# Attention scores of two head pairs in a row, and one pool of four accumulator banks, in a talking-heads attention, MoE and MLP kernel

## The chip, the cores and the metric

One core of a Trainium2 chip runs the whole kernel. The metric is device time in microseconds (us) of one execution; lower is better. Every instruction of an engine runs in the order in which the program holds it, so an engine that has to wait for one instruction also holds up all those behind it. TensorE (PE in the profile) multiplies into eight accumulator banks (PSUM); VectorE (DVE) and ScalarE (ACT) read the banks; SyncE's queue (SP) issues most DMAs.

## The reference

Three stages, one after the other. The change lies in the first.

```python
def _attn_ref(q, k, v, w_pre, w_post):            # B, H, S, D = 4, 12, 448, 64
    scores = np.matmul(q, k.transpose(0, 1, 3, 2)) / np.sqrt(64)
    scores = np.einsum('bhij,hg->bgij', scores, w_pre)      # heads mixed before
    attn = softmax(scores)                                   # max, exp, sum, divide
    attn = np.einsum('bhij,hg->bgij', attn, w_post)          # heads mixed after
    return np.matmul(attn, v)
# x = rows of all heads, (1792, 768); then
# moe:  expert = argmax(x @ w_gate) of 8; y = gate * relu(x @ w1[e]) @ w2[e]
# mlp:  h = y @ w_in; out = (h * cos(h)) @ w_out
```

## The kernel before

The attention works on 16 chunks `X` of queries: each of the four batches has three chunks of 120 rows and one of 88 (`CH`, L23). For a chunk, `qk(X, j)` makes the scores of the head pair `j` (heads 2j and 2j+1). Q and K are held transposed, one head of the pair on partitions 0 to 63 and the other on 64 to 127, each split into a high and a low part, so a pair takes six matmuls of 448 columns: three products (`KH,QH`, `KL,QH`, `KH,QL`), each for the two halves of the partitions, into two banks of the pool `pq`. Two copies (`brought`, L501) bring them to `SB[X]` in SBUF. A chunk has six such pairs.

When all twelve heads of a chunk lie there, blocks of ten rows (nine at the end) are taken with a DMA (`relay`, L258) that puts 10 rows x 12 heads on 120 partitions. A block is then mixed (`m`, L460, two matmul instructions since fp32 takes two), reduced (`nm`, L463), exponentiated (`E`, L467), scaled through the second mixing matrix (`kr`, L470 to L475), and mixed again and turned at once (`pa`, L481, eight instructions); a copy (L484) collects it in `AT`. There are 180 blocks. After a chunk's last block come its products with V (`px`, L304, two halves of 48 instructions), their transposes to rows (`pt`, L363), and for groups of chunks the gate logits (`pl`, L333) and the counting for the routing (`pq`, `plead`, L137). At the end of each batch the next batch's K and Q are turned (`heads`: `tp`, L183, then casts L515 and L517). Background pieces (`f`, `sq`, L1519 to L1535) narrow the MLP's weights beside it all.

The order of the attention's work on PE, DVE, ACT and SP is written out by a planner, `Plan`, when the kernel is built. Tasks are generators whose steps say which engine they run on and for how long, which slots they take and give (`q`, `m`, `o`, `v` are accumulator banks, two of each; `x` and `E` are SBUF buffers, five and three) and which events they need. `Plan.run` always takes the step that can start first, and among those that can start within 0.02 us on that engine the one of lowest rank. A step's instructions are put out in that order and stay in it. Scores take two `q` slots at once (`score`), and each copy gives one back; V products, transposes, logits and counting take `v`; a head's transposes take `q`. Tasks of scores have a rank some four to ten blocks ahead of the chunk that needs them.

Before the plan starts, a written-out prologue turns the first batch's K and Q (`turned`, with banks of three pools in turn) and makes the scores of chunk 0. After it, `between` runs the last chunk's products beside the first expert's.

Of the kernel before, what the change touches and what calls it, by code (L numbers as in the profile page):

```python
# [47 lines left out]
class Plan:  # L48
# [10 lines left out]
    def __init__(self, slots):  # L59
        self.free = {t: [0.0] * n for t, n in slots.items()}  # L60
        self.at, self.engine, self.pending = {}, {}, []
        self.now = self.reached = 0.0

    def add(self, rank, task, bg=False):
# [23 lines left out]
    def run(self):  # L88
        while self.pending:
            options = []  # L90
            for i, (order, rank, task, bg, t, step) in enumerate(self.pending):
                r = self.ready(t, step)
                if r is None:
                    continue
                for e, (hold, lat) in step["run"].items():
                    options.append((max(r, self.engine.get(e, 0.0)), order, hold, i, e, r, bg and rank > self.reached))
            assert options, [p[5] for p in self.pending]
            pick = None
            for o in sorted(options):
                start, order, hold, i, e, r, bg = o  # L100
                if bg and any(p[4] == e and not p[6] and p[5] < start + 0.7 * hold for p in options):
                    continue
                pick = o
                break
            pick = pick or min(options)

            start, e = pick[0], pick[4]
            same = [o for o in options if o[4] == e and o[0] <= start + 0.02 and (not o[6] or pick[6])]
            start, order, hold, i, e, r, bg = min(same, key=lambda o: (o[1], o[0]))
            order, rank, task, bg, t, step = self.pending.pop(i)  # L110
            hold, lat = step["run"][e]
            for tag in step.get("take", ()):
                self.free[tag].pop(0)
            self.now = start
            self.engine[e] = start + hold
            end = start + lat
            for tag in step.get("give", ()):
                self.free[tag] = sorted(self.free[tag] + [end])
            self.reached = max(self.reached, step.get("reached", 0.0))
            for ev in step.get("ends", ()):  # L120
                self.at[ev] = end
            self.go(rank, task, bg, end + self.HOP, e)

# [18 lines left out]
def attention(ctx, qctx, tc, q, k, v, w_pre, w_post, wg, xs, lg, ident, nb=4, side=None, route=None):  # L142
# [10 lines left out]
    sm = ctx.enter_context(tc.tile_pool(name="a_sm", bufs=4))  # L153
    pq = ctx.enter_context(tc.tile_pool(name="p_q", bufs=2, space=PS))
    pm = ctx.enter_context(tc.tile_pool(name="p_m", bufs=2, space=PS))
    po = ctx.enter_context(tc.tile_pool(name="p_o", bufs=2, space=PS))
    pv = ctx.enter_context(tc.tile_pool(name="p_v", bufs=2, space=PS))
    bal = Balance(nc)
# [18 lines left out]
    def turned(b, j, s, cs=slice(0, 4)):  # L177

        src = (KN, QN)[s][b, j]
        pool, tag = ((pm, "m"), (po, "o"), (pv, "v"))[(2 * j + s if cs.start == 0 else j) % 3] if b == 0 else (pq, "q")  # L180
        ps = pool.tile([128, 512], F32, tag=tag, name=f"tp{b}_{j}_{s}_{cs.start}")
        for c in range(4)[cs]:
            nc.tensor.transpose(ps[:, c * 112 : c * 112 + 112], src[:, c].rearrange("p a d -> p (a d)"), ident[:112, :112])  # L183
        return ps
# [70 lines left out]
    def relay(n):  # L255
        X, be, rs, m, M = geom(n)
        XR[n] = sk.tile([120, S], F32, tag="x", name=f"x{n}", bufs=5)
        nc.sync.dma_start(out=XR[n][:M], in_=SB[X][rs])  # L258

    def premix(n):  # L260
# [4 lines left out]
        nc.vector.reduce_max(nm[:M], ps[:M, :S], axis=AX.X, negate=True)  # L265
        e = wk.tile([120, S], F32, tag="E", name=f"E{n}", bufs=3)
        sg = sm.tile([120, 1], F32, tag="sg", name=f"sg{n}")
# [27 lines left out]
    def av_mm(X, half):  # L295
        b, c = chunks[X]
        n = CH[c][1]
        px = pv.tile([128, 3, 128], F32, tag="v", name=f"px{X}_{half}")
        for pr in range(3):
            for cc in range(4):  # L300

                for e in range(2):
                    g = 2 * (3 * half + pr) + e
                    nc.tensor.matmul(px[64 * e : 64 * e + 64, pr, :n], VN[b, g // 3][:, g % 3, cc], AT[X][:, cc, g, :n], start=(cc == 0), stop=(cc == 3))  # L304
        return px
# [21 lines left out]
    def logits_mm(Xs):  # L327

        pl = pv.tile([128, 512], F32, tag="v", name=f"pl{Xs[0]}")
        for cc in range(6):  # L330
# [12 lines left out]
    def logit_tiles(X):  # L343

        b, c = chunks[X]
        new = []
# [3 lines left out]
        if new:  # L350
            pt = pv.tile([128, 512], F32, tag="v", name=f"plt{X}")
            for i, t in enumerate(new):
                nc.tensor.transpose(pt[:, 8 * i : 8 * i + 8], LT[:, t * 128 % (2 * S) :][:, :128], ident[:8, :8])
            nc.vector.tensor_copy(lg[:, new[0] : new[-1] + 1].rearrange("p t e -> p (t e)"), pt[:, : 8 * len(new)])
            if route is not None:
                for t in new:
                    route.ready(t, pv, "v")

    def rows_mm(X, half):
        n = CH[chunks[X][1]][1]  # L360
        pt = pv.tile([128, 3, 128], F32, tag="v", name=f"pt{X}_{half}")
        for cc in range(3):
# [28 lines left out]
    def repeat():  # L391

        wps = pv.tile([128, 512], F32, tag="v", name="wps")
        nc.tensor.matmul(wps[:120, :24], rep.rearrange("p i h -> p (i h)"), wpp.rearrange("p j g -> p (j g)"), start=True, stop=True)
# [55 lines left out]

    plan = Plan({"q": 2, "m": 2, "o": 2, "v": 2, "x": 5, "E": 3, "kr": 4, "Sb": 1, "AT": 1, "W": 2, "sq": 2, "f": 2, "kn": 2, "qn": 2, "xr": 1, "xc": 4, "vn": 0})

    def block(n):
# [10 lines left out]
        yield dict(run={"ACT": (0.63, 0.76)}, later=-4, take=["E"], give=["m"])  # L464
        e = wk.tile([120, S], F32, tag="E", name=f"E{n}", bufs=3)
        sg = sm.tile([120, 1], F32, tag="sg", name=f"sg{n}")
# [21 lines left out]
    def score(X, j):  # L488
        b, c = chunks[X]
        on = [("K", b, j), ("Q", b, j)]  # L490
        if X >= 2:
            on += [("x", k) for k in range(first_of[X - 2], end_of[X - 2] + 1)]
        if j:
            on.append(("s", X, j - 1))
        yield dict(run=pe(0.7), take=["q", "q"], on=on, ends=[("s", X, j)])
        SC[X, j] = qk(X, j)

# [5 lines left out]
    def heads(b, j, s_):  # L503

        tag, src, t = (("kn", k, KN), ("qn", q, QN))[s_]
        yield dict(run=dma(4.0), take=[tag])
        load_pair(b, j, sk.tile([112, 4, 2, D], F32, tag=tag, name=f"{tag}{b}_{j}"), src, t)
        yield dict(run=pe(0.38), take=["q"], on=[("s", 4 * b - 1, j)])
# [15 lines left out]
    def products(X):  # L524
# [3 lines left out]
        for half in range(2):  # L528
            yield dict(run=pe(0.02 * n + 0.21), on=ats + [("V", b)], take=["v"] + (["xc"] if half == 0 else []), give=["AT"] if half else [], ends=[("av", X, half)])
            px = av_mm(X, half)  # L530
            eng = yield dict(run=copying(3 * n), give=["v"], ends=[("xc", X)] if half else [])
            av_out(X, half, px, by[eng])
        for half in range(2):
            yield dict(run=pe(0.33), take=["v"] + (["xr"] if half == 0 else []))
            pt = rows_mm(X, half)
            eng = yield dict(run=copying(384), give=["v"])
            rows_out(X, half, pt, by[eng])
# [3 lines left out]
    def gates(Xs):  # L541
        yield dict(run=pe(0.75), take=["v"], on=[("xc", X) for X in Xs])
        pl = logits_mm(Xs)
        for i, X in enumerate(Xs):
            b, c = chunks[X]
            i0, n, _ = CH[c]
            t0 = b % 2 * S + i0
            eng = yield dict(run=copying(n), give=["v"] if X == Xs[-1] else [])
            by[eng](LT[:, t0 : t0 + n], pl[32 * i : 32 * i + 8, :n])
# [3 lines left out]
        while state[0] is not None and (state[0] + 1) * 128 <= b * S + CH[c][0] + CH[c][1]:  # L553
            new.append(state[0])
            state[0] = next(tiles, None)
        yield dict(run=pe(0.1 * len(new)), take=["v"])
        pt = pv.tile([128, 512], F32, tag="v", name=f"plt{X}")
        for i, t in enumerate(new):
            nc.tensor.transpose(pt[:, 8 * i : 8 * i + 8], LT[:, t * 128 % (2 * S) :][:, :128], ident[:8, :8])
        yield dict(run=dve(0.2), give=["v"], ends=[("gates", X), ("xcs", X)])  # L560
        nc.vector.tensor_copy(lg[:, new[0] : new[-1] + 1].rearrange("p t e -> p (t e)"), pt[:, : 8 * len(new)])
        for t in new:
            if t >= NT - 1:
                continue
            kept, real = [], route.nc
            yield dict(run=dve(0.17), take=["v"])
            route.nc = Taken(real, kept)
            route.count(t, pv, "v")
            route.nc = real
            kept[0][1]()  # L570
            for i, (e, emit) in enumerate(kept[1:]):
                yield dict(run={"DVE": dve(0.2), "PE": pe(0.06)}[e][e] and ({"DVE": (0.12, 0.19)} if e == "DVE" else pe(0.06)), give=["v"] * (1 if t != TE - 1 else 2) if i == len(kept) - 2 else [])
                emit()
# [26 lines left out]
    for X in range(1, len(chunks)):  # L600
        n0, nb0 = first_of[X], CH[chunks[X - 1][1]][2]
        for j in range(H // 2):
            r = n0 - 4 - 8 * (X % 4 == 3) - (H - 2 - 2 * j) * (nb0 - 5) / H
            plan.add(r, score(X, j))
            for i in range(2):
# [1108 lines left out]
```

## Time and profile before

| | us |
|---|---|
| median of 3 runs | 1356.49 (1356.41 to 1357.92) |
| profiled execution, device time | 1357.03 |
| its span, first to last instruction | 1355.3 |
| attention's planned part, in the span | about 28 to 528 |
| PE busy in the span | 1323.2 (98%) |
| DVE busy | 1057.3 (78%) |
| ACT busy | 817.0 (60%) |

What lies around the span (1357.03 less 1355.3) is 1.7 us. PE's granted clock is at full speed from beginning to end (0.998 on average). A busy PE counts the modelled ends of matmuls that overlap, so the distances between starts say more than the busy time does.

### The profile page before, as it was taken

Reading aid. Unit: us, or ns where it says so; the run is one execution under the profiler, and the core shown is the slowest. Engines: PE = TensorE matmul, PEld = TensorE weight load, DVE = VectorE, ACT = ScalarE, POOL = GpSimd, SP = SyncE. Lnnn points to the kernel's source line nnn. Section 1 sums busy time; section 2 is a strip of 40 time slices with the busy share of each in tenths; the row PEclk is TensorE's granted clock in tenths of the full one; section 3 lists DMA queues with packets and bytes.
Section 4 is the critical chain, followed back from the end, with each engine's and each line's share of the span. In section 5 each row is a group of like instructions: output and inputs, shape, how many; then the busy total and the mean of one; then the engine's idle time right before and its main releaser. Section 6 shows DMA issues by size and latency. Waiting matters only on the chain.

```text
span 1355.3 us, 24788 instructions
## 1 busy us (share of the span) xinstructions
PE 1323.2 (98%) x8826; PEld 1079.0 (80%) x8826; DVE 1057.3 (78%) x2418; ACT 817.0 (60%) x1501; POOL 71.1 (5%) x67
## 2 busy tenths in 40 slices
PE   7999999999989999899999999999999999999997
PEld 4667676776767777799999999998888888888886
DVE  6877788788877887899999999897766666666663
ACT  5456565666656555788888889865444444444432
POOL 1000000000000000210000010011100020002001
PEclk9999999999999999999999999999999999999999
DMA  8558655865657557259465774365333343324201
GB/s 185 192 170 216 214 186 170 222 220 179 184 154 230 179 188 250 69 178 374 149 208 186 254 259 175 106 226 182 122 111 109 101 143 109 99 94 140 93 24 47
DMA packets 153280, 227.02 MB, mean 168 GB/s; under 512 B 55744, under 2 KB 115392, under 8 KB 153152
## 3 DMA queue, kind: packets, MB, share of 16 engines
q1 hardware_dynamic: 146816, 200.20, 46.0%
q0 software_dynamic: 3744, 18.09, 3.9%
q10 hardware_dynamic: 2592, 7.08, 1.3%
q8 instruction: 73, 1.20, 0.4%
q14 instruction: 55, 0.45, 0.1%
HBM read 217.87 MB, written 31.85 MB: 184 GB/s over the span
## 4 chain that ended last, share of the span: by engine, by line
PE 57%; DVE 0%; ACT 0%; issue 0%; POOLq 0%; POOL 0%; ACTq 0%
PE dh L1462 17%; PE op L1406 17%; PE yp L1221 10%; PE h L1187 10%; PE ph L1208 1%; PE px L1115 1%; PE dpt L1343 1%; ACT wh L1026 0%; DVE wl L1027 0%; POOLq L1709 0%; POOL out_dram L1415 0%; ACT dhs L1466 0%; ACT r L1429 0%; DVE xl L1125 0%; PE gspg L964 0%
## 5 line engine op out<-in xcount | busy, mean ns | idle before, releaser
L1027 DVE TENSOR_TENSOR wl<-r,wh 128x768 fp32r<-128x768 f32 (+1 forms) x246 | 249.1, 1060 | 13.3 <-ACT wh L1026 10.4
L1026 ACT CAST wh<-r 128x768 fp32r<-128x768 f32 (+1 forms) x246 | 224.0, 930 | 39.2 <-PE h L1187 30.3
L481 PEld LDWEIGHTS pa<-kr,E 120*112 120x112 f32 (+1 forms) x1440 | 164.6, 177 | 51.0 <-issue 36.5
L481 PE MATMUL pa<-kr,E 120*112 120x120 f32 (+1 forms) x1440 | 182.7, 270 | 3.3 <-DVE kr L475 2.6
L460 PE MATMUL m<-x,kpre 120*120 120x448 f32 x360 | 167.2, 557 | 1.0 <-ACT E L467 1.0
L1027 DVE TENSOR_TENSOR wil<-wi,wih 128x768 fp32r<-128x768 f32 x64 | 60.9, 952 | 134.1 <-ACT wih L1026 134.1
L1026 ACT CAST wih<-wi 128x768 fp32r<-128x768 f32 x64 | 53.7, 841 | 159.1 <-PE dh L1462 158.0
L463 DVE TENSOR_REDUCE nm<-m 120x1 f32<-120x448 f32 x180 | 111.6, 620 | 43.0 <-PE m L460 35.2
L467 ACT ACTIVATE E<-m,nm 120x448 f32<-120x448 f32 x180 | 114.5, 636 | 50.2 <-DVE nm L463 25.7
L1406 PE MATMUL op<-woh,gh 128*128 128x512 f32 x448 | 115.2, 338 | 0.0
L1406 PE MATMUL op<-woh,gl 128*128 128x512 f32 x448 | 114.6, 336 | 0.0
L1406 PE MATMUL op<-wol,gh 128*128 128x512 f32 x448 | 114.4, 336 | 0.0
L1462 PE MATMUL dh<-dxh,wih 128*128 128x512 f32 (+1 forms) x384 | 112.8, 369 | 0.0
L1462 PE MATMUL dh<-dxl,wih 128*128 128x512 f32 (+1 forms) x384 | 112.4, 367 | 0.0
L1462 PE MATMUL dh<-dxh,wil 128*128 128x512 f32 (+1 forms) x384 | 111.6, 367 | 0.0
L304 PEld LDWEIGHTS px<-AT,vn 112*64 112x64 f32 x1536 | 73.8, 137 | 14.9 <-issue 9.9
L1026 ACT CAST woh<-wo 128x768 fp32r<-128x768 f32 x64 | 53.3, 834 | 53.6 <-PE op L1406 51.4
L484 ACT COPY AT<-pa 112x480 f32<-112x480 f32 (+1 forms) x104 | 59.1, 569 | 39.4 <-PE pa L481 35.8
L1462 PEld LDWEIGHTS dh<-dxl,wih 128*128 128x128 f32 x384 | 70.2, 189 | 13.1
L304 PE MATMUL px<-AT,vn 112*64 112x120 f32 (+1 forms) x1536 | 80.4, 261 | 0.0
L1462 PEld LDWEIGHTS dh<-dxh,wil 128*128 128x128 f32 x384 | 69.8, 189 | 13.1
L501 ACT COPY S<-s 120x448 f32<-120x448 f32 (+1 forms) x104 | 54.3, 531 | 42.3 <-PE s L241 41.8
(276 smaller groups left out, 2575.0 us busy)
## 6 DMA issues: line engine op xcount, KB each, us to landing
r<-in_moe_w_dram SPq DMA_DIRECT2D x54, 1024.0 KB
r<-in_moe_w_dram SPq DMA_DIRECT2D x72, 768.0 KB
x<-S SPq DMA_DIRECT2D x172, 210.0 KB
wi<-wi SPq DMA_DIRECT2D x32, 768.0 KB
wo<-wo SPq DMA_DIRECT2D x32, 768.0 KB
W<-in_moe_w_in_dram SPq DMA_DIRECT2D x32, 384.0 KB
W<-in_moe_w_out_dram SPq DMA_DIRECT2D x32, 384.0 KB
ys<-y ACTq DMA_DIRECT2D x17, 384.0 KB
```

Source lines behind the costliest of these rows:

```text
L304: nc.tensor.matmul(px[64 * e : 64 * e + 64, pr, :n], VN[b, g // 3][:, g % 3, cc], AT[X][:, cc, g, :n], start=(cc == 0), stop=(cc == 3))
L460: nc.tensor.matmul(ps[:M, :S], kpre[:M, :M], x[:M], start=True, stop=True)
L463: nc.vector.reduce_max(nm[:M], ps[:M, :S], axis=AX.X, negate=True)
L467: last["act"] = nc.scalar.activation(e[:M], ps[:M, :S], AF.Exp, bias=nm[:M], scale=1.0, accum_out=sg[:M])
L481: nc.tensor.matmul(pa[:112, c, :120], e[:M, c * 112 : c * 112 + 112], kr[:M], start=True, stop=True)
L484: last["post"] = by[eng](AT[X][:, :, :, j0 : j0 + m], pa[:112, :, :120].rearrange("p c (g i) -> p c g i", i=10)[:, :, :, :m])
L1026: self.latest["A"] = nc.scalar.copy(hi, src).ins
L1027: self.latest["V"] = nc.vector.tensor_tensor(lo, src, hi.bitcast(F32), op=ALU.subtract).ins
L1187: self.nc.tensor.matmul(hp[n], a[:, k], w[:, n * 512 : n * 512 + 512], start=(k == 0 and i == 0), stop=(k == 5 and i == 2))
L1221: self.nc.tensor.matmul(yp[n][:, :384], a[:, k], w[:, n * 384 : n * 384 + 384], start=(k == 0 and i == 0), stop=(k == 7 and i == 2))
L1406: nc.tensor.matmul(bank[:, to], g[:, t * P : t * P + P], w[:, of], start=first, stop=(f == 15 and i == 2), skip_group_check=(n == 1))
L1462: nc.tensor.matmul(hp[:, :N], w[:, k], x[:, k, :N], start=(k == 0 and i == 0), stop=(k == 5 and i == 2))
```

## The change

Four things.

1. Scores are made by a task for two head pairs, `j` and `j + 1`, with two steps. The first step is planned as 0.9 us, the second as 0.6 us if it follows the first directly on PE (`then`). `Plan` remembers the task whose first step PE ran last (`self.row`) and gives that task's second step the lead among the PE steps that can start at once. Where its two banks aren't free at that moment, another PE step goes in between and the second pair runs alone, as before. The task now needs K and Q of both pairs.
2. The pool `pv` is gone; `pq` has four banks, for scores, turned heads, V products, transposes, logits and counting alike. `between` takes its banks there too.
3. The prologue's turned tiles use the pools `pm` and `po` in turn, four banks, and not the six of `pm`, `po` and `pv`.
4. The relayed blocks `x` have six buffers and not five, the exponentials `E` four and not three.

```diff
@@ Plan
+        self.row = None
...
-            start, order, hold, i, e, r, bg = min(same, key=lambda o: (o[1], o[0]))
+            start, order, hold, i, e, r, bg = min(same, key=lambda o: (e != "PE" or self.pending[o[3]][2] is not self.row, o[1], o[0]))
             order, rank, task, bg, t, step = self.pending.pop(i)
             hold, lat = step["run"][e]
+            if e == "PE":
+                if self.row is task:
+                    hold, lat = step["then"], step["then"] + lat - hold
+                self.row = task if "then" in step and self.row is not task else None
...
-            self.go(rank, task, bg, end + self.HOP, e)
+            self.go(rank, task, bg, start + hold if self.row is task else end + self.HOP, e)
@@ attention
-    pq = ctx.enter_context(tc.tile_pool(name="p_q", bufs=2, space=PS))
+    pq = ctx.enter_context(tc.tile_pool(name="p_q", bufs=4, space=PS))
...
-    pv = ctx.enter_context(tc.tile_pool(name="p_v", bufs=2, space=PS))
@@ turned
-        pool, tag = ((pm, "m"), (po, "o"), (pv, "v"))[(2 * j + s if cs.start == 0 else j) % 3] if b == 0 else (pq, "q")
+        pool, tag = ((pm, "m"), (po, "o"))[(s if cs.start == 0 else j) % 2] if b == 0 else (pq, "q")
@@ relay, block
-        XR[n] = sk.tile([120, S], F32, tag="x", name=f"x{n}", bufs=5)
+        XR[n] = sk.tile([120, S], F32, tag="x", name=f"x{n}", bufs=6)
-        e = wk.tile([120, S], F32, tag="E", name=f"E{n}", bufs=3)
+        e = wk.tile([120, S], F32, tag="E", name=f"E{n}", bufs=4)
@@ the planner's slots; every take and give of "v" becomes "q", every pv a pq
-    plan = Plan({"q": 2, "m": 2, "o": 2, "v": 2, "x": 5, "E": 3, ...})
+    plan = Plan({"q": 4, "m": 2, "o": 2, "x": 6, "E": 4, ...})
@@ score(X, j)
-        on = [("K", b, j), ("Q", b, j)]
+        on = [(t, b, i) for t in "KQ" for i in (j, j + 1)]
...
-        yield dict(run=pe(0.7), take=["q", "q"], on=on, ends=[("s", X, j)])
-        SC[X, j] = qk(X, j)
+        for i in (j, j + 1):
+            yield dict(run=pe(0.9), then=0.6, take=["q", "q"], on=on, ends=[("s", X, i)])
+            SC[X, i] = qk(X, i)
@@ the tasks of scores
-            plan.add(r, score(X, j))
+            if j % 2 == 0:
+                plan.add(r, score(X, j))
```

## Rows read from the trace of the kernel before

**Rows 1.** The page, part 1: span, and each engine's busy us, share and instructions

```profile
span 1355.3 us, 24788 instructions
...
PE 1323.2 (98%) x8826; PEld 1079.0 (80%) x8826; DVE 1057.3 (78%) x2418; ACT 817.0 (60%) x1501; POOL 71.1 (5%) x67
```

**Rows 2.** Stages of the planned attention: window, us, busy us (x) of PE, PEld, DVE, ACT, POOL

```profile
28.00:528.00 500.00, 489.06 (x4242) 351.55 (x4243) 399.67 (x1316) 293.97 (x723) 1.21 (x2) 1.00 0.63 194
28.00:148.00 120.00, 115.51 (x929) 81.70 (x928) 96.94 (x282) 69.66 (x171) 0.00 (x0) 1.00 0.63 191
```

**Rows 3.** Waits of PE from 28 to 528 us, longest first: us, times, longest

```profile
PE tp L183 <- DMA qn<-in_q_dram: 2.7, 2, 2.4
PE pa L481 <- DVE kr L475: 2.6, 3, 1.6
```

**Rows 4.** Timeline of PE, 200 to 206 us: start, us, line, out<-in, xcount

```profile
200.62 1.76 PE L460 MATMUL m<-x,kpre 120*120 120x448 f32 x4
202.22 0.98 PE L481 MATMUL pa<-kr,E 120*112 120x120 f32 x8
203.13 0.47 PE L241 MATMUL s<-KH,QH 64*120 64x448 f32 x2
203.44 0.37 PE L241 MATMUL s<-KL,QH 64*120 64x448 f32 x2
203.64 0.37 PE L241 MATMUL s<-KH,QL 64*120 64x448 f32 x2
203.94 1.07 PE L481 MATMUL pa<-kr,E 120*112 120x120 f32 x8
204.85 0.92 PE L460 MATMUL m<-x,kpre 120*120 120x448 f32 x2
205.70 0.43 PE L241 MATMUL s<-KH,QH 64*88 64x448 f32 x2
```

**Rows 5.** Timeline of PE's weight loads at the same pair of heads

```profile
203.23 0.18 PEld L241 LDWEIGHTS s<-KL,QH 64*120 64x120 f32 x2
```

**Rows 6.** Groups by line, 28 to 528 us: the copies of scores; busy us, mean ns, idle before

```profile
L501 ACT COPY S<-s 120x448 f32<-120x448 f32 (+1 forms) x101 | 52.7, 531 | 39.5 <-PE s L241 39.0
L501 DVE COPY S<-s 120x448 f32<-120x448 f32 (+1 forms) x74 | 45.9, 621 | 12.6 <-PE s L241 9.1 <-DMA qn<-in_q_dram 1.0
```

**Rows 7.** Timeline of all engines at the plan's beginning, 21 to 28 us

```profile
21.39 1.37 PE L183 MATMUL tp<-ident,fq 112*128 112x112 f32 x12
...
22.21 1.88 DVE L202 TENSOR_TENSOR QL<-tp,QH 128x224 fp32r<-128x224 f32 x6
...
22.69 0.47 PE L241 MATMUL s<-KH,QH 64*120 64x448 f32 x2
...
24.18 0.46 PE L241 MATMUL s<-KH,QH 64*120 64x448 f32 x1 [0.62 <-ACT S L501]
...
26.26 0.75 PE L241 MATMUL s<-KH,QH 64*120 64x448 f32 x2 [0.42 <-ACT S L501]
...
27.35 1.76 PE L460 MATMUL m<-x,kpre 120*120 120x448 f32 x4
```

**Rows 8.** Timeline of all engines around one counting tile, 187 to 194 us

```profile
187.97 0.18 PE L137 MATMUL pq<-ohb,tri 128*128 128x8 bf16 x1
...
188.94 2.68 PE L304 MATMUL px<-AT,vn 112*64 112x120 f32 x48
...
193.28 0.49 PE L363 MATMUL pt<-ident,xc 128*120 128x128 f32 x3
...
193.48 0.29 DVE L137 TENSOR_TENSOR pa<-pq,pa 112x128 f16<-112x128 f32 x1 [0.18 <-PE pq L137]
```

**Rows 9.** Timeline of SP's queue at the end of the attention

```profile
516.65 0.33 SPq L1535 DMA_DIRECT2D wo<-f  x1
517.20 1.99 SPq L1091 DMA_DIRECT2D r<-in_moe_w_dram  x3
```

More of the change, by code (lines that the diff above doesn't have):

```diff
@@ L297, in av_mm @@
         n = CH[c][1]
-        px = pv.tile([128, 3, 128], F32, tag="v", name=f"px{X}_{half}")
+        px = pq.tile([128, 3, 128], F32, tag="q", name=f"px{X}_{half}")
         for pr in range(3):
@@ L327, in logits_mm @@
     def logits_mm(Xs):
-        pl = pv.tile([128, 512], F32, tag="v", name=f"pl{Xs[0]}")
+        pl = pq.tile([128, 512], F32, tag="q", name=f"pl{Xs[0]}")
         for cc in range(6):
@@ L350, in logit_tiles @@
         if new:
-            pt = pv.tile([128, 512], F32, tag="v", name=f"plt{X}")
+            pt = pq.tile([128, 512], F32, tag="q", name=f"plt{X}")
             for i, t in enumerate(new):
@@ L356, in logit_tiles @@
                 for t in new:
-                    route.ready(t, pv, "v")
+                    route.ready(t, pq, "q")
     def rows_mm(X, half):
         n = CH[chunks[X][1]][1]
-        pt = pv.tile([128, 3, 128], F32, tag="v", name=f"pt{X}_{half}")
+        pt = pq.tile([128, 3, 128], F32, tag="q", name=f"pt{X}_{half}")
         for cc in range(3):
@@ L391, in repeat @@
     def repeat():
-        wps = pv.tile([128, 512], F32, tag="v", name="wps")
+        wps = pq.tile([128, 512], F32, tag="q", name="wps")
         nc.tensor.matmul(wps[:120, :24], rep.rearrange("p i h -> p (i h)"), wpp.rearrange("p j g -> p (j g)"), start=True, stop=True)
@@ L449, in dma @@
         return {"SP": (0.8, d)}
-    plan = Plan({"q": 2, "m": 2, "o": 2, "v": 2, "x": 5, "E": 3, "kr": 4, "Sb": 1, "AT": 1, "W": 2, "sq": 2, "f": 2, "kn": 2, "qn": 2, "xr": 1, "xc": 4, "vn": 0})
+    plan = Plan({"q": 4, "m": 2, "o": 2, "x": 6, "E": 4, "kr": 4, "Sb": 1, "AT": 1, "W": 2, "sq": 2, "f": 2, "kn": 2, "qn": 2, "xr": 1, "xc": 4, "vn": 0})
     def block(n):
@@ L464, in block @@
         yield dict(run={"ACT": (0.63, 0.76)}, later=-4, take=["E"], give=["m"])
-        e = wk.tile([120, S], F32, tag="E", name=f"E{n}", bufs=3)
+        e = wk.tile([120, S], F32, tag="E", name=f"E{n}", bufs=4)
         sg = sm.tile([120, 1], F32, tag="sg", name=f"sg{n}")
@@ L506, in heads @@
         yield dict(run=dma(4.0), take=[tag])
-        load_pair(b, j, sk.tile([112, 4, 2, D], F32, tag=tag, name=f"{tag}{b}_{j}"), src, t)
+        load_pair(b, j, sk.tile([112, 4, 2, D], F32, tag=tag, name=f"{tag}{b}_{j}", bufs=2), src, t)
         yield dict(run=pe(0.38), take=["q"], on=[("s", 4 * b - 1, j)])
@@ L528, in products @@
         for half in range(2):
-            yield dict(run=pe(0.02 * n + 0.21), on=ats + [("V", b)], take=["v"] + (["xc"] if half == 0 else []), give=["AT"] if half else [], ends=[("av", X, half)])
+            yield dict(run=pe(0.02 * n + 0.21), on=ats + [("V", b)], take=["q"] + (["xc"] if half == 0 else []), give=["AT"] if half else [], ends=[("av", X, half)])
             px = av_mm(X, half)
-            eng = yield dict(run=copying(3 * n), give=["v"], ends=[("xc", X)] if half else [])
+            eng = yield dict(run=copying(3 * n), give=["q"], ends=[("xc", X)] if half else [])
             av_out(X, half, px, by[eng])
         for half in range(2):
-            yield dict(run=pe(0.33), take=["v"] + (["xr"] if half == 0 else []))
+            yield dict(run=pe(0.33), take=["q"] + (["xr"] if half == 0 else []))
             pt = rows_mm(X, half)
-            eng = yield dict(run=copying(384), give=["v"])
+            eng = yield dict(run=copying(384), give=["q"])
             rows_out(X, half, pt, by[eng])
@@ L541, in gates @@
     def gates(Xs):
-        yield dict(run=pe(0.75), take=["v"], on=[("xc", X) for X in Xs])
+        yield dict(run=pe(0.75), take=["q"], on=[("xc", X) for X in Xs])
         pl = logits_mm(Xs)
@@ L547, in gates @@
             t0 = b % 2 * S + i0
-            eng = yield dict(run=copying(n), give=["v"] if X == Xs[-1] else [])
+            eng = yield dict(run=copying(n), give=["q"] if X == Xs[-1] else [])
             by[eng](LT[:, t0 : t0 + n], pl[32 * i : 32 * i + 8, :n])
@@ L555, in gates @@
             state[0] = next(tiles, None)
-        yield dict(run=pe(0.1 * len(new)), take=["v"])
-        pt = pv.tile([128, 512], F32, tag="v", name=f"plt{X}")
+        yield dict(run=pe(0.1 * len(new)), take=["q"])
+        pt = pq.tile([128, 512], F32, tag="q", name=f"plt{X}")
         for i, t in enumerate(new):
             nc.tensor.transpose(pt[:, 8 * i : 8 * i + 8], LT[:, t * 128 % (2 * S) :][:, :128], ident[:8, :8])
-        yield dict(run=dve(0.2), give=["v"], ends=[("gates", X), ("xcs", X)])
+        yield dict(run=dve(0.2), give=["q"], ends=[("gates", X), ("xcs", X)])
         nc.vector.tensor_copy(lg[:, new[0] : new[-1] + 1].rearrange("p t e -> p (t e)"), pt[:, : 8 * len(new)])
@@ L565, in gates @@
             kept, real = [], route.nc
-            yield dict(run=dve(0.17), take=["v"])
+            yield dict(run=dve(0.17), take=["q"])
             route.nc = Taken(real, kept)
-            route.count(t, pv, "v")
+            route.count(t, pq, "q")
             route.nc = real
@@ L571, in gates @@
             for i, (e, emit) in enumerate(kept[1:]):
-                yield dict(run={"DVE": dve(0.2), "PE": pe(0.06)}[e][e] and ({"DVE": (0.12, 0.19)} if e == "DVE" else pe(0.06)), give=["v"] * (1 if t != TE - 1 else 2) if i == len(kept) - 2 else [])
+                yield dict(run={"DVE": dve(0.2), "PE": pe(0.06)}[e][e] and ({"DVE": (0.12, 0.19)} if e == "DVE" else pe(0.06)), give=["q"] * (1 if t != TE - 1 else 2) if i == len(kept) - 2 else [])
                 emit()
```

## The prediction

> **What bounds the kernel now.** I read the page's busy shares first: PE is busy for 98% of the span, DVE for 78% [rows 1]. Then the stages: from 28 to 528 us, the planned attention, PE is busy for 489.1 of 500 us, DVE for 399.7, ACT for 294.0 [rows 2]. With 180 blocks in it that is 2.78 us a block, of which PE fills 2.72, DVE 2.22 and ACT 1.63. PE would have to lose about a fifth of its work before DVE could set the pace. Next PE's waits in that stage: the longest sums are 2.7 us for DMAs of the next batch's Q and 2.6 us for `kr` [rows 3]; no long sum is a wait for an accumulator bank. So what PE loses there lies inside its own stream, and the view that shows it is the timeline of starts.
>
> There one pair of heads stands between a `pa` and a `pa` [rows 4]: its three products start at 203.13, 203.44 and 203.64, and the next work at 203.94. The middle product takes 0.20 us, the first 0.31, the last 0.30. So 0.81 us are spent on what would be 0.60 at the pace of the middle step. The entry costs a bit more: `m` before scores takes 0.85 (204.85 to 205.70), while two `m` before a `pa` take 1.60 together (200.62 to 202.22), 0.80 each; a `pa` before scores takes 0.91 (202.22 to 203.13), no more than the 0.91 before an `m` (203.94 to 204.85). The planner of before had two banks for scores, so a pair always stood alone: all 87 pairs from 28 us on pay this.
>
> **The change, part by part.**
>
> *Two pairs in a row.* If the second pair runs at the middle step's pace through its entry, and the first pair's exit too, the pair of pairs saves the excess of one first step (0.11), of one last step (0.10) and, where the second pair would have stood behind an `m`, that entry's 0.05, say half the time: 0.24 us. Nothing in the trace shows two pairs in a row, so bounds. From below: if the second pair's first loads can't run ahead, its first step stays at 0.31 and 0.13 is saved. From above 0.26, with the `m` entry every time. I take 0.24, since within a pair each product's loads already run while the product before streams: the loads for the second product start at 203.23, 0.10 us after the first matmul and 0.21 before their own [rows 4, 5].
>
> A rule that speaks against this: the Trainium skill, TensorE: Matmul & The Clock Gate, section "Part 3: Packing small matmuls — row/col tiling", says that a weight load overlaps a running matmul only when it goes to another group of rows. By that rule the second pair's first load would wait for the half it goes into, the price would be the lower bound, and the time that of the third rival below; the row at 203.23 speaks against it, as both halves are streaming then.
>
> *How many.* There are 15 planned chunks with three pairs of pairs each, 45; three of them are chunk 1's, counted with the beginning below, so 42. Each second pair needs two more free banks just when the first ends. What else holds banks: scores until their copies are done (0.53 us on ACT, 0.62 on DVE, two at once [rows 6]); a half of V's products for 2.6 us and its copy (188.94 to 191.55 by the distance to the next start; the row at 188.94 lasts 2.68); a counting tile from 187.97 to 193.77, 5.8 us [rows 8], of which there are 13. With one tile of another kind in use three banks are left, and the second pair must wait or go alone. Blocks leave about 5 us between two pairs of pairs, long enough for the four copies. I estimate 85% in a row, 36; bounds 50% and 100%. Sum: 36 x 0.24 = 8.6 us, all of it on PE, which is the path here.
>
> *Four banks at the beginning.* After the prologue PE makes chunk 1's scores and waits for copies: pairs start at 22.69, 24.18 and 26.26 us, and the first `m` at 27.35 [rows 7]. Three pairs at 0.81 fill 2.4 of 4.7 us. With four banks one to three more pairs fit into the 2.3 us of gaps, or the first `m` comes earlier, where its DMA allows. I take 1.5 us, bounds 0 and 2.5.
>
> *Fewer banks for the prologue.* The six late transposes (21.39 to 22.69) go into four banks, so the fifth waits for the first's reader on DVE, which starts at 22.21 and takes 0.31 each (1.88 for six) [rows 7]. PE would be held to about 22.9 with chunk 1's scores and the first `m` queued behind it. The 2.3 us of gaps hide that; without them it would cost 0.3 to 0.6 us. I take 0.
>
> *One pool for all.* Does a counting tile block the tiles behind it when banks are shared? It need not, as one stretch shows [rows 8]: with two banks in `pv`, both the half of V's products at 188.94 and the transposes at 193.28 run while the counting tile is still held (its last reader starts at 193.48). So a bank is taken as it comes free, not in turn. Cost 0; the other case is the slower rival.
>
> *More `x` and `E` buffers.* They can only take away waits, and PE is idle for 10.9 us in the stage [rows 2]. The named waits are for Q's DMA and `kr` [rows 3]; neither needs these buffers. I take 0, bounds 0 and 3 us of gain. SP's queue issues the same DMAs; relays may go out one earlier.
>
> *What comes after.* The first expert's weights are issued at 517.20, right after SP's last piece of the attention at 516.65 [rows 9]: they hang on the attention's order, not on a time of their own, and come forward with it. After that, PE is the chain that ends last, so the gain arrives in full.
>
> Sum: 8.6 + 1.5 = 10.1 us. The profiled execution's 1357.0 becomes 1346.9; it stands 0.5 above the median, so I forecast 1346.5. Ends: 21 x 0.13 = 3 us, and 42 x 0.26 + 2.5 + 3 = 16.4 us.
>
> **The rivals.**
>
> *Few in a row.* The change may not do what it says. If V's halves, turned heads and counting hold a bank whenever a pair of pairs comes up, a third of the 42 are in a row: 14 x 0.24 + 1.5 = 4.9 us, 1351.6. For it speaks that all four banks must be free or about to be; against it that scores are planned blocks ahead and can choose their moment.
>
> *The gain is given back.* The order of everything is planned anew, and PE keeps to it. Where PE waits for DMAs, as in the first 120 us of the stage with 4.5 us idle [rows 2], being earlier is worth nothing. If half the gain is lost there and the 10.9 us of idle time become 15, the gain is 1 us: about 1355.5.
>
> *No load ahead.* The lower price: 36 x 0.13 + 1.5 = 6.2 us, 1350.3.
>
> *Slower: PE stands for banks.* Some 110 tiles that had `pv` or `pq` with little company (30 halves, 30 transposes, 36 turned heads, 13 countings) now share with 45 pairs of pairs that take all four banks. PE's order is fixed by planned durations; where a copy comes later than planned, PE stands with `m` and `pa` of the next blocks behind it, and DVE and ACT then stand for those. Such a wait can be as long as one copy, 0.53 to 0.62 us [rows 6]. It decides from a mean of 0.12 us a tile (13 us, more than the gain and 2.7). At 0.15, 16.5 us go and the time is 1357 - 10 + 16.5 = 1363. Against it: at most 10.9 us were idle with two banks of each kind, and a shared pool of four gives each kind more than it had on average. The Trainium skill, TensorEngine Tiling, section "Gotcha 1: PSUM Pressure", warns of just this: row tiles raise the pressure on the banks.
>
> **How the numbers follow.** Forecast 0.55, at 1340.5 to 1350; no load ahead 0.10; few in a row 0.13; given back 0.11; slower 0.11. A measurement of this kernel can tell about 0.2%, 2.7 us, from no change. The first three are faster: 0.78. Given back is within: 0.11. Slower: 0.11. The range holds the first three and about half of the fourth: from 1340 (about the upper end of the gain, 16.4 us) to 1355.5.
>
> **What would show it.** In the timeline after: twelve score matmuls in a row with starts 0.20 us apart across the seam (right), or 0.31 again (no load ahead). The count of such rows: 36 or so of 45, or a third. PE's waits: no sum of more than 3 us with `S` copies or `xc` copies as the releaser; if those grow to over 10 us, the slower rival holds. At the beginning: no wait for `S` between 22 and 27 us. The distance from the first `m` to the first expert's first hidden matmul should shrink by 8 to 10 us, and all behind it stay as it is. The prediction is wrong if that distance doesn't shrink, or if it does and the end doesn't follow.

## The result, and the profile after

| | us |
|---|---|
| before, median of 4 | 1356.61 |
| after, median of 4 (1339.77 to 1346.05) | 1343.28 |
| ratio, 95% interval | 0.9893 (0.9878 to 0.9909) |
| profiled execution after, device time | 1346.05 |
| its span | 1343.3 |

The kernel is 13.3 us faster by the medians. The profiled execution of after is the longest of its four, 11.0 us under the profiled one of before; the readings below are from it. Its span is 12.0 us shorter; what lies around the span is 2.7 us here and was 1.7 in before. One execution of all, of the kernel before in another order, took 7434 us and is left out of the ratios.

Page of after, part 1, as [rows 1]:

```profile
span 1343.3 us, 24789 instructions
...
PE 1312.6 (98%) x8826; PEld 1084.1 (81%) x8826; DVE 1056.0 (79%) x2427; ACT 814.1 (61%) x1492; POOL 74.0 (6%) x67
```

PE's busy time has fallen by 10.6 us, DVE's by 1.3 and ACT's by 2.9. Timeline of PE in after around two tasks of scores (start, us, line, out<-in, xcount), as [rows 4]:

```profile
44.64 0.46 PE L245 MATMUL s<-KH,QH 64*120 64x448 f32 x2
44.94 0.37 PE L245 MATMUL s<-KL,QH 64*120 64x448 f32 x2
45.14 0.36 PE L245 MATMUL s<-KH,QL 64*120 64x448 f32 x2
45.35 0.36 PE L245 MATMUL s<-KH,QH 64*120 64x448 f32 x2
45.55 0.37 PE L245 MATMUL s<-KL,QH 64*120 64x448 f32 x2
45.75 0.36 PE L245 MATMUL s<-KH,QL 64*120 64x448 f32 x2
46.05 1.07 PE L485 MATMUL pa<-kr,E 120*112 120x120 f32 x8
46.96 0.92 PE L464 MATMUL m<-x,kpre 120*120 120x448 f32 x2
47.71 0.98 PE L485 MATMUL pa<-kr,E 120*112 120x120 f32 x8
48.53 0.92 PE L464 MATMUL m<-x,kpre 120*120 120x448 f32 x2
...
53.25 0.92 PE L464 MATMUL m<-x,kpre 120*120 120x448 f32 x2
54.10 0.47 PE L245 MATMUL s<-KH,QH 64*120 64x448 f32 x2
```

Two pairs take 1.41 us (44.64 to 46.05), where two single ones took 1.62. The seam, 45.14 to 45.35, runs at the middle step's pace: the loads for the matmuls at 45.35 start at 45.15, while both halves stream.

```profile
45.15 0.18 PEld L245 LDWEIGHTS s<-KH,QH 64*120 64x120 f32 x2
```

And there is more to read here than the prediction read. The `pa` right behind scores takes 0.91 (46.05 to 46.96), the `pa` between two `m` 0.82 (47.71 to 48.53). The `m` between two `pa` takes 0.75 (46.96 to 47.71), the `m` ahead of scores 0.85 (53.25 to 54.10). So each change between the half-height tiles of the scores (64 of the array's 128 rows, 64*120 in their rows) and full-size work costs 0.09 us in the neighbour too, on the way in and on the way out.

In the planned part of after, 30 of 42 tasks have their pairs in a row and 12 do not; chunk 1's three tasks all stand ahead of the first `m`. Timeline of PE at the beginning of after, as [rows 7]:

```profile
22.48 0.56 PE L245 MATMUL s<-KH,QH 64*120 64x448 f32 x2
...
24.16 0.46 PE L245 MATMUL s<-KH,QH 64*120 64x448 f32 x1 [0.43 <-DVE S L506]
...
24.67 0.56 PE L245 MATMUL s<-KH,QH 64*120 64x448 f32 x2
...
26.26 0.56 PE L245 MATMUL s<-KH,QH 64*120 64x448 f32 x2
...
27.16 1.01 PE L464 MATMUL m<-x,kpre 120*120 120x448 f32 x2
```

Six pairs are made by 27.16 us, where before made three by 27.35. PE still stands for a copy of scores once, 0.43 us at 24.16. PE's waits from 28 to 518 us in after (us in total, times, longest), as [rows 3]:

```profile
PE tp L187 <- DMA qn<-in_q_dram: 6.1, 4, 3.4
PE m L464 <- DMA x<-S: 1.5, 1, 1.5
...
PE s L245 <- DVE l L142: 0.7, 1, 0.7
...
PE s L245 <- ACT S L506: 0.4, 1, 0.4
```

The waits for banks are short. The long one is for the landing of Q of the last batch, 3.4 us in one piece, more than in before (2.4).

To set work against waits I summed distances between starts for the planned part, from the first `m` to the end of the last `pa` of a block. The work, called own work below, is counted at the undisturbed distances: 180 blocks at 0.754 + 0.820; a half of V's products 2.61 (1.97 in short chunks); turned heads 0.385, transposes 0.33, logits 1.34; a pair alone 0.80 (0.77 in short chunks), two in a row 1.41 (1.38 in short chunks); and 0.094 for each change between full-size work and scores, V's products or logits. V's products are half as wide (112*64 in their rows) and logits 8 columns wide (128*8); a `pa` ahead of logits takes 0.914 and an `m` ahead of V's products 0.845, as ahead of scores. The small matmuls of the counting, 2 to 3 us in all, are in it too. What is left of the stretch is put down as wait, slower work at a lower clock included.

| profiled execution of | pairs, and runs of two | changes | own work, us | waits, us | last `pa` ends at |
|---|---|---|---|---|---|
| before | 87, 0 | 218 | 480.6 | 18.8 | 526.8 |
| after | 84, 30 | 164 | 467.1 | 22.0 | 516.3 |

The own work falls by 13.5 us: the three pairs that the beginning has taken in (0.80 and two changes each, 3.0) and 30 pairs in a row (10.5, so 0.35 each). The waits grow by 3.2, most of it slower work at a lower clock (2.8 us, shown in the last section). From the first hidden matmul of the first expert to the MLP's first it is 328.3 us before and 326.8 after, a further 1.5 us gained.

### The profile page after: what moved, and what is told of

Its sections match the earlier page's. It is cut to its first block, busy times and chain, and to the rows that moved or that the text cites. A ratio compares the mean times of both kernels' runs of the same rounds, so it can differ in the third digit from the quotient of the medians.

```text
span 1343.3 us, 24789 instructions
## 1 busy us (share of the span) xinstructions
PE 1312.6 (98%) x8826; PEld 1084.1 (81%) x8826; DVE 1056.0 (79%) x2427; ACT 814.1 (61%) x1492; POOL 74.0 (6%) x67
## 4 chain that ended last, share of the span: by engine, by line
PE 58%; DVE 1%; issue 0%; ACT 0%; POOLq 0%; POOL 0%; ACTq 0%
PE dh L1468 17%; PE op L1412 17%; PE yp L1227 11%; PE h L1193 10%; PE ph L1214 1%; PE px L1121 1%; PE dpt L1349 1%; DVE wl L1033 0%; ACT wh L1032 0%; POOLq L1715 0%; POOL out_dram L1421 0%; ACT dhs L1472 0%; ACT r L1435 0%; DVE xl L1131 0%; PE gspg L970 0%
## 5 line engine op out<-in xcount | busy, mean ns | idle before, releaser
L485 PEld LDWEIGHTS pa<-kr,E 120*112 120x112 f32 (+1 forms) x1440 | 167.8, 178 | 47.4 <-issue 32.9
L488 ACT COPY AT<-pa 112x480 f32<-112x480 f32 (+1 forms) x99 | 56.3, 569 | 49.8 <-PE pa L485 46.4
L1468 PEld LDWEIGHTS dh<-dxh,wih 128*128 128x128 f32 x384 | 68.5, 189 | 12.9 <-ACT dhs L1472 0.3
```

What stands on the lines that cost most here:

```text
L485: nc.tensor.matmul(pa[:112, c, :120], e[:M, c * 112 : c * 112 + 112], kr[:M], start=True, stop=True)
L488: last["post"] = by[eng](AT[X][:, :, :, j0 : j0 + m], pa[:112, :, :120].rearrange("p c (g i) -> p c g i", i=10)[:, :, :, :m])
L1468: nc.tensor.matmul(hp[:, :N], w[:, k], x[:, k, :N], start=(k == 0 and i == 0), stop=(k == 5 and i == 2))
```

## The experiments

Ratios are each against runs of the kernel before on the same chip in the same job; 1% is 13.6 us.

**The seam broken.** Is it the array's change of tiles, or only the order? A small matmul over the full height (128 rows, 8 columns) is put ahead of every second pair of a task, 45 in all; 30 of them stand in the seams of the planned part, 12 ahead of second pairs that ran alone. The written order is the same.

```diff
+        if X and j % 2:
+            nc.tensor.matmul(ps[0][:8, 448:456], ident[:, :8], ident[:, :8], start=True, stop=True)
```

> The changed kernel in the same written order, with one full-height matmul of 8 columns put ahead of every second pair of a task (45 in all), into columns of that pair's bank that nobody reads. So the pairs still follow each other, but the array leaves the half-height tiles for a moment. Theory (leaving and entering the half-height tiles costs about 0.2 us inside a pair and 0.09 on either side): each of the 30 seams of the planned part loses about 0.39 us and the small matmul's own 0.1, 12 to 16 us in all, about 1357 to 1360 us on this chip, where the changed kernel took 1344. Rival (a pair in a row is cheap because it needs no wait, whatever the array does between): 45 x 0.1 = 4.5 us at most, under 1349 us.

Measured: 1352.17 us, ratio 0.9962 (0.9947 to 0.9977), where the changed kernel has 0.9892 (0.9874 to 0.9909) when run again: 0.0070, 9.5 us, of the 14.7 are given back. PE's timeline of this kernel at the task that began at 44.64 in after:

```profile
43.73 0.46 PE L247 MATMUL s<-KH,QH 64*120 64x448 f32 x2
...
44.23 0.37 PE L247 MATMUL s<-KH,QL 64*120 64x448 f32 x2
44.53 0.20 PE L244 MATMUL s<-ident 128*8 128x8 f32 x2
44.66 0.47 PE L247 MATMUL s<-KH,QH 64*120 64x448 f32 x2
44.96 0.37 PE L247 MATMUL s<-KL,QH 64*120 64x448 f32 x2
...
45.46 1.07 PE L487 MATMUL pa<-kr,E 120*112 120x120 f32 x8
```

The task takes 1.73 us, 0.32 more than in after: the first step is 0.30 again, the last step 0.30, and the small matmul 0.13; each pair takes 0.80, as a pair alone does. 30 seams x 0.32 are 9.6 us, and the 12 other small matmuls add 1.6. The time lost 9.5 us (the two intervals leave some 3 us to either side). That lies between the two expectations: under the theory's 12 to 16, which had put 0.49 on a seam, and over the rival's 4.5. The rows decide for the theory's kind, as the steps at the seam are long again. In the profiled execution the last `pa` ends only 4.9 us later than in after, as its waits are shorter, about 15 us and not 22. A half-height matmul in the seam was not run; against the view that any other matmul there would cost as much stands that work of full size with other weights costs its neighbour nothing: an `m` ahead of a `tp` takes 0.754 in before, as ahead of a `pa`.

**Single pairs, all else kept.** The task for two is undone; four banks, prologue and buffers stay.

```diff
@@ score(X, j), now for one pair; each j has its own task again
-        for i in (j, j + 1):
-            yield dict(run=pe(0.9), then=0.6, take=["q", "q"], on=on, ends=[("s", X, i)])
-            SC[X, i] = qk(X, i)
+        yield dict(run=pe(0.7), take=["q", "q"], on=on, ends=[("s", X, j)])
+        SC[X, j] = qk(X, j)
```

> The changed kernel, but each head pair is a task of its own again (0.7 us, two banks), so the lead for a second pair is gone; the pool of four banks, the prologue and the buffers stay as changed. In its written order 2 of the pairs of pairs still stand in a row, not 30. Theory (a change between pairs in half-height tiles and full-height work costs on both sides, and a pair in a row saves 0.39 us: 0.21 inside the pair, 0.09 on the work before it, 0.09 on the work behind it): 28 x 0.39 = 11 us are given back, about 1354 us, 2 us under the kernel before for the pairs that the beginning still takes in. Rival (the four shared banks, the buffers and the new order bring the gain): 1343 to 1346 us.

Measured: 1348.09 us, ratio 0.992 (0.9907 to 0.9933), 10.9 us under before and 4 us over the changed kernel in the same job. Neither was right: the pairs in a row were worth 4 us here, not 11, and the rest of the change 11, not 2. The 11 us of PE work did come back (478.5 us of own work against 467.1 in the next table), but the waits were shorter.

**Banks alone, buffers alone.** What brings 11 us with single pairs? Once only the pool and the prologue (single pairs as above and the old buffers), once only the buffers on the kernel before.

```diff
@@ buffers alone, on the kernel before; the planner's x and E slots likewise
-        XR[n] = sk.tile([120, S], F32, tag="x", name=f"x{n}", bufs=5)
+        XR[n] = sk.tile([120, S], F32, tag="x", name=f"x{n}", bufs=6)
-        e = wk.tile([120, S], F32, tag="E", name=f"E{n}", bufs=3)
+        e = wk.tile([120, S], F32, tag="E", name=f"E{n}", bufs=4)
```

> Single pairs as before and the buffers of x and E as before (five and three): of the change only the pool of four banks and the prologue on two pools are left, and the order that the planner makes of them; no two pairs in a row after the beginning. With single pairs and the added buffers the time was 1348.1 us, 11 us under the kernel before. Theory: the four banks and what the order makes of them (five pairs of chunk 1 ahead of the first mixing and not three, fewer waits at the turns of batches) give that: 1346 to 1351 us. Rival: the added buffers gave it: 1355 us or more.

> The kernel before with six x and four E buffers, all else as before. Theory: the buffers give nothing, 1355 to 1361 us as the kernel before. Rival: they give most of the 11 us that single pairs with the new pool and buffers had: under 1352 us.

Measured: pool alone 1350.79 us, ratio 0.9963 (0.9948 to 0.9977), 5.0 us; buffers alone 1349.4, ratio 0.995 (0.9933 to 0.9966), 6.8 us. For the pool the theory holds (1346 to 1351). For the buffers it falls: they do gain, by themselves. Both nearly keep PE's own work and lose waits:

| profiled execution of | pairs, and runs of two | changes | own work, us | waits, us | last `pa` ends at |
|---|---|---|---|---|---|
| pool alone | 85, 0 | 219 | 479.1 | 13.7 | 519.9 |
| buffers alone | 87, 0 | 212 | 480.0 | 13.5 | 520.3 |
| single pairs, pool and buffers | 85, 2 | 218 | 478.5 | 16.1 | 521.5 |
| after, run again | 84, 30 | 164 | 467.1 | 21.3 | 514.7 |
| after with the old buffers | 84, 32 | 157 | 466.1 | 19.4 | 512.1 |

**The old buffers in the changed kernel.** Five `x` and three `E`; all else as changed.

```diff
@@ the planner's slots; bufs of the x and E tiles likewise
-    plan = Plan({"q": 4, "m": 2, "o": 2, "x": 6, "E": 4, ...})
+    plan = Plan({"q": 4, "m": 2, "o": 2, "x": 5, "E": 3, ...})
```

> The changed kernel with five x and three E buffers, as before. Its written order has 32 pairs of pairs in a row (30 in the changed kernel). Theory: no buffer was waited for, so the time stays at 1340 to 1346 us. Rival (the added buffers bring part of the gain): over 1347 us, with PE waiting for E or x.

Measured: 1342.23 us, ratio 0.9887 (0.9869 to 0.9904), the changed kernel's within the intervals, as the theory had it. Here the buffers bring nothing. This kernel and the pool alone differ by the pairs in a row and the order written with them, 0.9887 against 0.9963: 10.3 us. With the buffers in both, the same step is worth 4 (0.992 to 0.9892). Each of the two differences is known to some 3 us only, and in the profiled executions the last `pa` comes 7.8 and 6.8 us earlier; that of the single pairs was the slowest of its six, 3.1 us over their median. So that the step is worth less with the buffers is likely, but at the limit of what these runs tell. Buffers and banks take waits away and pairs in a row take work from PE, and in these orders, with PE's own work 11 to 13 us shorter, its waits are 19 to 22 us and not 13 to 16. Of the waits of after, 2.8 us are the lower clock, and 3.3 of those of after run again.

**Is it a matter of the order alone?** One planned duration is changed, which writes another order of the same work; twice for each kernel: 4.4 and 4.0 in before, 4.6 and 4.0 in after. The edit to 4.0:

```diff
-        yield dict(run=dma(4.2), take=["x"], on=[("S", X, h) for h in range(H)], ends=[("x", n)])
+        yield dict(run=dma(4.0), take=["x"], on=[("S", X, h) for h in range(H)], ends=[("x", n)])
```

> The kernel before with one number of the planner changed: a block's relay is planned as 4.4 us and not 4.2. Same work, same 87 single pairs, same banks and buffers; only the written order differs. Theory (the kernel before has about 5 us of waits more than the orders of the pool-only and buffers-only kernels, and those are a matter of the order, not of banks or buffers): another order loses or gains several us, and the time is 1349 to 1355 us, with PE's waits of the planned part 3 to 6 us below those of before. Rival (banks and buffers themselves gave the 5 to 7 us): within 2 us of the kernel before.

> As the last, with the relay planned as 4.0 us: a second other order of the kernel before. Theory: 1349 to 1356 us, not the same as the last one. Rival: within 2 us of the kernel before.

> The changed kernel with the relay planned as 4.6 us: 29 pairs of pairs in a row and not 30. Theory: PE's own work stays, less one pair (0.3 us); the waits of the order differ by some us, so 1340 to 1348 us on a chip where the changed kernel takes 1344. Rival (its order was a lucky one): over 1350 us.

> The changed kernel with the relay planned as 4.0 us: 31 pairs of pairs in a row, but two pairs fewer ahead of the first mixing. Theory: 1340 to 1348 us, about 1.5 us of it for the two pairs at the beginning. Rival (its order was a lucky one): over 1350 us.

Measured: before with 4.4, 1357.32 us, ratio 0.9994 (0.9976 to 1.0012), waits 17.8; with 4.0, 1357.81, ratio 0.999 (0.9973 to 1.0007), waits 17.4. So my theory falls: three orders of the kernel before have 17 to 19 us of waits and the same time, so it was not an unlucky order of before that the banks or the buffers mended, and the rival holds. Pool alone, buffers alone and single pairs were each run in one order only; what another order of theirs would give is not shown. After with 4.6: 1341.93 us, ratio 0.9882 (0.9857 to 0.9908); with 4.0: 1338.85 us, ratio 0.986 (0.9836 to 0.9885), 19 us under before, the best of all and under the 1340 to 1348 that I expected. That one has 31 runs of two, own work of 468.9 us, and waits of 13.9. So the changed kernel's gain doesn't hang on one order, but its size differs by some 4 us between the three, and a better one exists: with waits as short as those of the pool alone, PE's shorter work arrives.

**Three loads for the next batch's K and Q.** Against the wait of 3.4 us.

```diff
@@ the planner's kn and qn slots likewise
-        load_pair(b, j, sk.tile([112, 4, 2, D], F32, tag=tag, name=f"{tag}{b}_{j}", bufs=2), src, t)
+        load_pair(b, j, sk.tile([112, 4, 2, D], F32, tag=tag, name=f"{tag}{b}_{j}", bufs=3), src, t)
```

> The changed kernel with three buffers, not two, for the K and for the Q of the next batch's head pairs, in the planner and in SBUF, so their DMAs can be issued earlier; 31 pairs of pairs stand in a row. Theory: PE's waits for kn and qn (6.5 us in the profiled execution of the changed kernel) go, the clock doesn't fall, and the times lie close together at 1336 to 1340 us. Rival (the spread comes from elsewhere): the waits go, the spread of 6 us stays, median 1340 to 1343.

Measured: 1342.43 us (1342.12 to 1344.13), ratio 0.9884 (0.9867 to 0.9901). The theory's 1336 to 1340 us did not come; the median is the rival's, but the spread fell to 2 us. The waits for Q are gone, all waits are 13.8 us, and the attention's last `pa` ends at 508.4 us, 8 us ahead of after. But the first expert's first hidden matmul is at 519.7, only 1.2 us ahead. POOL's row for the gather of the first expert's rows in this kernel, and PE's rows behind the last block:

```profile
505.38 1.03 POOL L1113 DMA_INDIRECT xg<-xs,ids  x1 [500.94 <-DMA r<-in_moe_w_dram]
```

```profile
512.71 1.54 PE L1121 MATMUL px<-ident,xg 128*128 128x128 f32 x6 [3.97 <-DMA xg<-xs,ids]
514.18 5.61 PE L308 MATMUL px<-AT,vn 112*64 112x88 f32 x96
```

The gather goes out at 505.4 us, in after at 496.3; the profile puts its wait down to the weights' DMA. PE stands 4.0 us for it, and from 511.0 its granted clock is at the lower level, 1.2 GHz, for 6.8 us: from start to start, the two steps above take 1.47 and 5.54 us, in after 0.76 and 3.79. So the gain was given back at the seam between attention and experts, by the wait and by 2.5 us of slower work behind it. Why the gather goes out so late here stays open.

**All four banks at once.** Every task's pairs in a row, by force.

```diff
-            yield dict(run=pe(0.9), then=0.6, take=["q", "q"], on=on, ends=[("s", X, i)])
+            yield dict(run=pe(0.9), then=0.6, take=["q"] * 4 if i == j else [], on=on, ends=[("s", X, i)])
```

> The changed kernel, with the first pair of a task planned to take all four banks, so that the second always follows it: 40 pairs of pairs and one row of six in the planned part, not 30 of 42; two pairs fewer are made ahead of the first mixing. Theory: PE's own work falls by 10 to 12 further joined pairs x 0.39 = 4 to 4.7 us, less 2 x 0.8 at the beginning: 1340 to 1343 us, if nothing new is waited for. Rival (the first pair now waits for four free banks and the blocks behind it wait too, or the weights and rows of the first expert come late and take the gain): 1344 us or more, with PE's waits longer or the first expert's rows waited for.

Measured: 1355.71 us, ratio 0.9986 (0.9973 to 0.9999): nearly the whole gain gone. PE's own work is 464.2 us with 86 pairs, less than after's with 84, but the waits are 35.5:

```profile
PE m L464 <- ACT E L471: 4.4, 5, 1.3
PE tp L187 <- DMA qn<-in_q_dram: 3.9, 3, 2.0
...
PE pq L142 <- DVE Le L142: 2.0, 2, 1.5
...
PE px L308 <- ACT AT L488: 1.5, 3, 0.7
```

The rival holds by the time and by the waits. Up to 5.1 us of the 35.5 are the lower clock, in two stretches of 10.2 us together; but executions with a mean granted clock of 0.998 and 0.999 took 1354 us too, so the clock is not the main cause. That it is the taking of all banks at once that holds back what shares them is the reading that fits; the list does not prove it, as most of its waits are for `E`, Q and the counting, and only 1.2 us for copies of scores.

**The spread of after.**

> The changed kernel once more, for the spread of its times (1339.8 to 1346.1 us in four executions, where the kernel before has 1.5 us). Theory: a wait of PE for a landing of Q at the turn of a batch (3.4 us at 363 us in the profiled execution) is at times so long that the granted clock falls to its lower level afterwards; executions with a mean granted clock of 0.998 take about 1340 us and those with 0.996 take 1342.5 to 1346. Rival: the times do not go with the clock.

Measured: 1344.11 us (1342.23 to 1345.31), ratio 0.9892 (0.9874 to 0.9909). A mean granted clock of 0.996 goes with 1344.3 and 1344.0 us, 0.997 with 1342.2 and 1345.3. The times don't go with the clock alone, and the kernel before spread by 5 us in this job. The theory isn't borne out, though falls of the clock do take part: this profiled execution has two, worth 3.3 us together.

## Why the prediction was right, and where its steps were off

The forecast, 1346.5 us, was 3.2 us above the median, and the profiled execution lost 11.0 us for 10.1 forecast. What bounds and the kind of gain were right. That the number came out so near is luck in part: PE's own work fell by 13.5 us where 10.1 was forecast, and waits that were put at nothing took 3.2 of it.

*What bounds.* Right: only PE's stream got shorter, and the end followed it.

*Two pairs in a row, 0.24 us.* The kind was right, the size wrong: 0.35, over my upper bound of 0.26. Inside the pair, 0.21 us (1.62 to 1.41) is what the forecast had, 0.11 and 0.10; the term that was too small is that of the neighbours. For these I had one price only, 0.05 for an `m` ahead of scores, and none for a `pa` [rows 4]. But the 0.91 that I took as the plain `pa` (203.94 to 204.85) belongs to one behind half-height tiles, and the other 0.91 (202.22 to 203.13) to one that goes ahead of them. Plain is 0.82, and a plain `m` 0.75 and not 0.80. So the neighbour pays 0.09 on the way in and 0.09 on the way out. Rows with plain neighbours were in the trace, and I did not look for them. The sentence of the Trainium skill that fits is in TensorEngine Tiling, section "Key Properties": a change of the tiling mode drains the array. It states no price; the rows do, 0.09 us on either side beside the 0.2 inside the pair. The rule of the Trainium skill that spoke against the change, in TensorE: Matmul & The Clock Gate, section "Part 3: Packing small matmuls — row/col tiling", on weight loads that overlap only when the group of rows differs, is not what this trace shows: at 45.15 the loads into both halves start while both halves stream, and the matmuls behind them start 0.20 us later. The rival that rested on it falls.

*How many.* 36 forecast, 30 came, and at a few of these the second pair still stood for a bank (0.7 us for `l`, 0.4 for a copy, in PE's waits). 30 x 0.35 is 10.5 us, 8.6 was forecast: two errors that partly cancel.

*Beginning.* Three pairs more in the same time, as the upper part of the range said. Worth 3.0 us and not 1.5, over the upper bound of 2.5, as each carries two changes of tiles. The sign that no copy would be waited for there did not come (0.43 us at 24.16). The late transposes did wait, and the gaps hid it: the first `m` came 0.2 us earlier.

*Waits, 0.* This was the step that failed most, though the sum hides it. By the medians, pool and buffers by themselves take 5 and 7 us, where I had 0, with 0 to 3 for the buffers. But with PE's work shorter the waits came back, to 22.0 us, 2.8 of it the lower clock. I had taken PE's idle time, 10.9 us, for all that waits cost; the sum of distances gives 18.8. The rest lies where PE counts as busy. Two rows of before show how:

```profile
112.25 0.92 PE L460 MATMUL m<-x,kpre 120*120 120x448 f32 x2
114.44 0.57 PE L183 MATMUL tp<-ident,kn 112*128 112x112 f32 x4 [1.27 <-DMA kn<-in_k_dram]
```

From start to start it is 2.19 us, a plain `m` takes 0.75, so 1.44 are lost, and 1.27 are listed: the row's modelled end, 0.92, lies 0.17 behind the place where the next work could start. In before 17 listed waits hide 3.1 us in this way. The other 5 us or so lie in distances that are a little too long without idle time; some stand beside the counting's small matmuls, where an `m` between two takes 0.83 us and not 0.75, and are then work and not wait. What makes the rest, no run shows. Which of these short waits the banks and the buffers end, the runs don't tell apart; that stays open.

*Slower rival.* It did not come with the change: PE's waits for copies of scores are 0.4 us in sum. The forced version comes near to it, with 35.5 us of waits and hardly a gain.

*After the attention, the gain in full.* Slightly more than that: 10.5 us at the first hidden matmul, 12.0 at the MLP's first. From the first `m` to that first hidden matmul it is 10.3 us less, where 8 to 10 were the sign. Part of what comes behind it: the transposes of the second expert's rows waited 1.7 us before and no longer wait. The three-loads kernel shows that being earlier by 8 us more at this seam brought 1.2.

## What to carry to other kernels

Where a kernel mixes matmuls on tiles of the array with full-size ones, count the changes between them and price one by the neighbours' distances as well as by its own: compare the same instruction with plain neighbours on both sides and with a tiled one on one side. Put tiled work in a row where it can go without waiting; forced, it lost the gain here. And judge a step that shortens the busiest engine by the waits that follow: here 11 to 13 us less work brought 4 us in one setting and 10 in another by the medians, each known to some 3 us.

## What the runs showed that I had not expected

After the wait of 3.4 us for Q, PE's granted clock went to its lower level, 1.2 GHz, for 6.8 us. Windows of after: us, busy (x) of PE, PEld, DVE, ACT and POOL, granted clock, DMA share, GB/s.

```profile
363.00:366.00 3.00, 0.53 (x2) 0.00 (x0) 2.73 (x10) 0.96 (x3) 0.00 (x0) 1.00 0.94 270
366.00:369.00 3.00, 2.10 (x11) 2.13 (x12) 0.00 (x0) 1.09 (x3) 0.00 (x0) 0.50 0.83 275
369.00:372.00 3.00, 3.00 (x11) 1.38 (x9) 1.15 (x4) 1.08 (x3) 0.00 (x0) 0.50 0.13 45
372.00:375.00 3.00, 3.00 (x19) 1.98 (x18) 2.36 (x8) 1.73 (x4) 0.00 (x0) 0.87 0.21 73
```

The pair of scores at 370.90 us took 1.40 us there, where it takes 0.80 at the full clock:

```profile
370.90 0.73 PE L245 MATMUL s<-KH,QH 64*120 64x448 f32 x2
371.43 0.57 PE L245 MATMUL s<-KL,QH 64*120 64x448 f32 x2
371.80 0.57 PE L245 MATMUL s<-KH,QL 64*120 64x448 f32 x2
372.30 1.30 PE L485 MATMUL pa<-kr,E 120*112 120x120 f32 x8
```

From 366.90 to 373.44 us PE did in 6.54 us what takes 3.77 by the distances at the full clock. So a wait of 3.4 us cost 2.8 more in slower work, and that much of after's 22.0 us of waits is the clock. The length of a wait alone does not decide it: before waited 2.4 us at the same turn and its clock stayed up, while in the second profiled execution of after the clock fell for 3.4 us each after waits of 2.1 and 2.6 us. In before the clock is not at full speed to the very end of the span: from 1350.2 us on, where PE has no more work, it is at the lower level, and it falls at the end of every other profiled execution too.
